# One order of tensor work in an attention, a third early slot in the expert layer behind it, and an earlier last turn in its small slots

## The chip, the cores and the metric

The kernel runs on one core of one Trainium2 chip. The metric is the device time of one execution in microseconds (us), taken as the median of several runs. The profile shows one more execution of the same program.

## The reference

An attention over buckets, and behind it a layer of eight experts of which each token uses one. For the attention there are 4 batches of 8 heads, 768 positions and 64 dimensions; each query and key gets a 6-bit bucket from the signs of a projection, and scores count only between equal buckets.

```
q_bits = einsum("bhsd,dk->bhsk", q, proj) > 0          # k_bits likewise; 6 bits make a bucket
scores = where(q_bucket == k_bucket, 0.125 * q @ k.T, -1e9)
scores = scores - max(scores)
attn   = exp(scores) / (sum(exp(scores)) + 1e-9)
x      = (attn @ v) as [3072 tokens, 512]
logits = x @ w_gate + modality_bias[modality_id]       # 8 experts
e      = argmax(logits);  gate_w = softmax(logits)[e]
out[t] = gate_w[t] * (relu(x[t] @ w1[e]) @ w2[e])      # w1: 512 x 1024, w2: 1024 x 512 per expert
```

All inputs are random and float32; the results are float32 too.

## The kernel before

**Attention.** The 32 heads are worked as 16 pairs, four pairs to a batch. For one pair, TensorE turns the loaded q and k (tiles n) to the layout that it multiplies, makes the hash bits, and adds to the turned q and k rows of patterns, so that a score of unequal buckets comes out far below the others. The work of the pair i is spread over six steps kt (blocks of 128 keys), and work for other pairs is woven in. In which order PE gets the pieces is written by hand: `PLAN` has a string for each kt, and a letter is one piece of work. The letters that matter here:

- S: one step of the scores of pair i (L306 and L307 into the PSUM tile pss, exponentials on ACT in L319 and L324 into pb). A: weighing of the values (L342 into psu).
- M: one step of the row maxima of pair i+1 (L240 into psm; DVE reduces it to mx in L242). B: its way back (L269, a turn into psx, and DVE's L271 and L272, which write m_1g and lone from it).
- T: one step of the chain for pair i+2: turns of n (L181, four 128 x 128 transposes into psx), signs (L208), patterns (L223). P: the same chain of the pair before.
- f, g, e, h, k: steps of `finish` of the last batch (normalisation, logits, routing). x, y: steps of `finish_x` (turn of the batch's result in L423, DVE's L425 into xs, a store of xs to the DRAM tile x_d in L427).

The pools of psx, psm and pss have two buffers each. A string's order is PE's order; the other engines are ordered by a scheduler.

**Routing.** When a batch's attention is done, `finish` computes logits and gates, and counts tokens by expert (L608 on PE, DVE's L590 to L627); POOL scatters (L630) token numbers and gates into the DRAM table tab, sorted by expert. Tokens are worked in slots: a big slot is 256 tokens of one expert, a small one 128. Slots that need only the first three batches are called early; their experts and offsets are in the table eslot, made by `early_slots()`. When all four batches are routed, `late_slots()` (L641 to L712) makes the tables bslot and sslot for the rest. `EARLY` is the number of early slots, `SURE_BIG` = 12 - EARLY the number of late big slots that run without a guard, and two small slots run without one. Further slots, if the tokens need them, run behind branches in `conditional`.

**A slot.** `Runner.slot` has eight steps j. At each, `ahead()` issues weight loads (SP, L747 for w1 and L749 for w2, 512 KB each into four raw buffers; up to seven steps ahead) and splits what has come in into a high and a low part (ACT casts in L755, DVE or POOL subtracts in L757, w with seven buffers). Each product is done as three matmuls of the parts. Steps 0 to 3 are the first product (L792 to L794 into hps, ACT's L798, DVE's L799), steps 4 to 7 the second (L834 to L836 into yps); at the end y is scaled (ACT, L841) and scattered to the output (POOL, L842).

A slot's tokens are fetched by `gather`: SP reads the slot's offset (L762) and issues a read of its part of tab into tb (L765); POOL, when tb is there, issues one gather for each 128 tokens (L769) from x_d into xg. `prepare` turns xg (L780, eight transposes for a big slot) and splits it into xh and xl (L781, L782). `prepare` of the next slot stands at j = 4; `fetch` of the next two slots (fd = 2) at j = 0 of every slot but the first.

In a small slot, the first product comes out with tokens in the partitions (L808 to L810), ACT makes hn (L812), and `turn_small` turns it (L818, two transposes), with a copy on ACT (L821, hh) and a subtraction on DVE (L822, hl). There are four turns, one step behind the products; the last is at j = 4.

`drive` weaves generators: the slot's eight steps, and beside them a given number of steps of another generator, spread over a given part. The small slots are at places 10 and 13 of the 14, counted from 0.

Of the kernel before, what the change touches and what calls it, by code (L numbers as in the profile page):

```python
# [9 lines left out]
F32 = mybir.dt.float32  # L10
# [4 lines left out]
ALU = mybir.AluOpType  # L15
# [3 lines left out]
B, H, S, D = 4, 8, 768, 64  # L19
# [3 lines left out]
REST = S - MAIN  # L23
NP = B * H // 2
BIG = 2.0 ** 100
CFG = dict(spd=(15,), fxs=3, wy=(0.3, 0.71), hpf=0, he=0, hn=0, hm=0, avp=(1, 2, 3, 4, 5, 6), avs=(2,), early=2, w3=(0, 0.9), x3=(0, 1), nmd=1, man=(), man0=2, hpo=0, hpe=0, p0=(0, 1), p1=(0, 0.25), p2=(0, 0.4), p3=(0.4, 0.9), s0=4, rc='DDDD', rq=(1, 2), tq=(3, 3, 1, 1, 0, 0), wh=(0.5, 0.78), ws=(0.78, 1.05), n2=2, psx=2, psm=2, pss=2, npb=4, ut=8, qk=3, v=2, wm=(0, 0.9), wf=(0.04, 1.02), wx=(0.3, 0.71), sub="DPPD", fx='D', fx3='R', raw=4, wp=7, LS=4, LL=7, pn=8, rv=(0,), rs='DDPP', r1=(0, 0.5), r2=(0, 1), avg=1, fub=2, fd=2, pm=(), fj=0, fxe=1.0)
P = 128

LAG = 2
PLAN = (  # L30
    "LvSPMTMSASfMTMfexyhk",
    "SMTVMSASfMTMeyghk",
    "SMTMSAQFGlSMTMEfxyk",
    "SMSATWSBMEekk",
# [23 lines left out]
def drive(gens):  # L58

    at = [0] * len(gens)  # L60
    alive = [True] * len(gens)
    while any(alive):
        j = min((x for x in range(len(gens)) if alive[x]), key=lambda x: gens[x][2] + (gens[x][3] - gens[x][2]) * (at[x] + 1) / gens[x][1])
        try:
            next(gens[j][0])
            at[j] += 1
        except StopIteration:
            alive[j] = False
# [7 lines left out]
def attention(ctx, actx, tc, a, x_d, l_d, route=None, setup=None):  # L76
# [4 lines left out]
    spool = ctx.enter_context(tc.tile_pool(name="spool", bufs=2))  # L81
    upool = ctx.enter_context(tc.tile_pool(name="upool", bufs=CFG["ut"]))
    bp = ctx.enter_context(tc.tile_pool(name="bp", bufs=1))
    ps_x = ctx.enter_context(tc.tile_pool(name="ps_x", bufs=CFG["psx"], space=PSUM))
    nat = actx.enter_context(tc.tile_pool(name="nat", bufs=CFG["n2"]))
    ld = actx.enter_context(tc.tile_pool(name="ld", bufs=CFG["qk"]))
    gens = []
    for g in range(3):
        opp = actx.enter_context(tc.tile_pool(name=f"opp{g}", bufs=1))
        gens.append({n: [opp.tile([P, S], F32R, name=f"{n}_{h}g{g}") for h in range(2)] for n in ("m1", "s1", "m2", "s2")})  # L90
    ldv = actx.enter_context(tc.tile_pool(name="ldv", bufs=CFG["v"]))
    sm = actx.enter_context(tc.tile_pool(name="sm", bufs=4))
    const = actx.enter_context(tc.tile_pool(name="const", bufs=1))
    ps_m = actx.enter_context(tc.tile_pool(name="ps_m", bufs=CFG["psm"], space=PSUM))
    ps_s = actx.enter_context(tc.tile_pool(name="ps_s", bufs=CFG["pss"], space=PSUM))
# [427 lines left out]
EARLY = CFG["early"]  # L523
# [194 lines left out]
def experts(ctx, tc, a, x_d, tab, out, ps_x, ident):  # L718
    nc = tc.nc
    w1, w2 = a["moe_w1"], a["moe_w2"]  # L720
    xp = ctx.enter_context(tc.tile_pool(name="xp", bufs=2))
    raw = ctx.enter_context(tc.tile_pool(name="raw", bufs=CFG["raw"]))
# [11 lines left out]
    def nt(s):  # L734
        return 1 if s[0] == "s" else 2
# [49 lines left out]
    def gemm1(hi, lo, xh, xl, hh, hl):  # L785
        hi = hi.rearrange("p (c f) -> p c f", c=4)
        lo = lo.rearrange("p (c f) -> p c f", c=4)
        for fb in range(2):
            fs = slice(fb * P, (fb + 1) * P)
            hps = ps_h.tile([P, TS], F32, name="hps")  # L790
            for c in range(4):
                nc.tensor.matmul(hps, lo[:, c, fs], xh[:, c], start=(c == 0), stop=False)  # L792
                nc.tensor.matmul(hps, hi[:, c, fs], xl[:, c], start=False, stop=False)  # L793
                nc.tensor.matmul(hps, hi[:, c, fs], xh[:, c], start=False, stop=(c == 3))  # L794
            th = hp.tile([P, TS], F32R, name="hh")
            tl = hp.tile([P, TS], F32R, name="hl")
            with tc.high_priority(offset=CFG["hpo"]):
                nc.scalar.activation(th, hps, AF.Relu)  # L798
                nc.vector.scalar_tensor_tensor(out=tl, in0=hps, scalar=0.0, in1=th.bitcast(F32), op0=ALU.max, op1=ALU.subtract)  # L799
            hh.append(th)  # L800
            hl.append(tl)
# [13 lines left out]
    def turn_small(h, hh, hl):  # L815
        tp = ps_h.tile([P, TS], F32, name="hps")
        for fb in range(2):
            nc.tensor.transpose(tp[:, fb * P:(fb + 1) * P], h[:, fb * P:(fb + 1) * P], ident)  # L818
        th = hp.tile([P, TS], F32R, name="hh")
        tl = hp.tile([P, TS], F32R, name="hl")  # L820
        nc.scalar.copy(out=th, in_=tp)  # L821
        nc.vector.tensor_tensor(out=tl, in0=tp, in1=th.bitcast(F32), op=ALU.subtract)  # L822
        for fb in range(2):
            hh.append(th[:, fb * P:(fb + 1) * P])
            hl.append(tl[:, fb * P:(fb + 1) * P])

    def gemm2(j, hi, lo, hh, hl, yps):
        hi = hi.rearrange("p (c f) -> p c f", c=2)
        lo = lo.rearrange("p (c f) -> p c f", c=2)
        for fb in range(2):  # L830
            fc = (j - 4) * 2 + fb
            for g in range(len(yps)):
                gs = slice(g * P, (g + 1) * P)
                nc.tensor.matmul(yps[g], hl[fc][:, gs], hi[:, fb], start=(fc == 0), stop=False)  # L834
                nc.tensor.matmul(yps[g], hh[fc][:, gs], lo[:, fb], start=False, stop=False)  # L835
                nc.tensor.matmul(yps[g], hh[fc][:, gs], hi[:, fb], start=False, stop=(fc == 7))  # L836
# [8 lines left out]
    class Runner:  # L845
# [35 lines left out]
        def slot(self, k):  # L881
            s = self.order[k]
            nxt = self.order[k + 1] if k + 1 < len(self.order) else None
            self.prepare(s)
            hh, hl, h = [], [], None
            for j in range(8):
                self.ahead()
                if j == CFG["fj"] and k > 0:
                    for s2 in self.order[k + 1:k + 1 + CFG["fd"]]:
                        self.fetch(s2)  # L890
                if j == 4:
                    yps = [ps_y.tile([P, DM], F32, name="yps") for _ in range(nt(s))]
                    if nxt:
                        self.prepare(nxt)
                hi, lo = self.ws.pop(self.n)
                if j >= 4:
                    gemm2(j, hi, lo, hh, hl, yps)
                elif nt(s) == 2:
                    gemm1(hi, lo, *self.xs[s], hh, hl)
                else:  # L900
                    last, h = h, gemm1_small(hi, lo, *self.xs[s])
                    if last is not None:
                        turn_small(last, hh, hl)
                if j == 4 and h is not None:
                    turn_small(h, hh, hl)
                self.n += 1
                yield
            store(self.got[s][0], yps)
# [22 lines left out]
def body(tc, a, out):  # L931
    nc = tc.nc
    x_d = tc.dram_tile([N + 1, DM], F32, name="x_d")
    tab = tc.dram_tile([DUMMY + TS, 2], I32, name="tab")
    with ExitStack() as ctx, ExitStack() as actx:
        route, early_slots, late_slots, setup = router(ctx, tc, a, x_d, tab)
        finish, finish_x, ps_x, ident = attention(ctx, actx, tc, a, x_d, None, route, setup)
        actx.close()
        runner, tabs, conditional = experts(ctx, tc, a, x_d, tab, out, ps_x, ident)
        r = runner()  # L940
        with tc.high_priority(offset=CFG["hpf"]):
            tabs["e"] = early_slots()
        r.extend([("e", i) for i in range(EARLY)])
        with tc.high_priority(offset=CFG["hpf"]):
            r.fetch(("e", 0))
        with tc.high_priority(offset=CFG["hpe"]):
            r.prepare(("e", 0))
        r.ahead()
        r.fetch(("e", 1))
        k = 0  # L950
        if EARLY > 2:
            drive([(r.slot(0), 8, 0, 1), (finish(B - 1), 14, *CFG["w3"])])
            drive([(r.slot(1), 8, 0, 1), (finish_x(B - 1, 0, NT), 12, *CFG["x3"])])
            k = 2
        else:
            for _ in finish(B - 1):
                pass
        tabs["b"], tabs["s"], tot = late_slots()
        late = [("b", i) for i in range(SURE_BIG)]
        for i in range(SURE_SML):  # L960
            late.insert(len(late) - 3 * i, ("s", i))
        r.extend(late)
        if EARLY == 2:
            drive([(r.slot(0), 8, 0, 1), (finish_x(B - 1, 0, NT), 12, 0, CFG["fxe"])])
            k = 1
        for k in range(k, len(r.order)):
            drive([(r.slot(k), 8, 0, 1)])
        conditional(tot)
# [13 lines left out]
```

## Time and profile before

| what | value |
|---|---|
| time, three runs | 877.72, 882.26, 884.44 us (median 882.26) |
| profiled execution | 876.72 us, span 874.9 us, mean granted TensorE clock 0.985 |
| PE busy | 817.9 us (93%) |
| DVE, ACT, POOL busy | 585.8, 506.0, 458.6 us |
| DMA | 110.87 MB, mean 127 GB/s |

The span is what the profiler saw between the first and the last instruction; the execution's time has 1.8 us around it. The attention lasts to about 535 us, and the 14 slots follow. In rows of the timeline the columns are start, duration, engine, line and operation, the result and its sources, shapes, the count, and in brackets the idle time before and what ended it. In rows of waits they are the waiting engine, tile and line, what it waited for, and total us, number, longest. SPq and POOLq are the queues in which SP and POOL issue their transfers.

### The profile page before, as it was taken

How to read it: one execution, taken by the hardware profiler on the slowest of the kernel's cores; microseconds unless marked ns; L12 is line 12 of the kernel's file. 1: busy time of each engine (PE TensorE's matmuls, PEld its weight loads, DVE VectorE, ACT ScalarE, POOL GpSimd, SP SyncE). 2: the span in 40 equal slices, each digit the busy share in tenths (PEclk: the TensorE clock that was granted, in tenths of full speed). 3: DMA queues.
4: the chain of work that ended last, by engine and by line, in shares of the span. 5: the costliest groups of instructions: out<-in, count | busy, mean ns of one | idle time of the engine just before them, and what ended most of it. 6: DMA issues, size and time to landing. Idle time of an engine off the chain costs nothing.

```text
span 874.9 us, 14548 instructions
## 1 busy us (share of the span) xinstructions
PE 817.9 (93%) x5154; PEld 579.5 (66%) x5154; DVE 585.8 (67%) x1029; ACT 506.0 (58%) x953; POOL 458.6 (52%) x347
## 2 busy tenths in 40 slices
PE   6799999999999999999999898879999999999993
PEld 3556555555555654555554555779999999998993
DVE  6776676676967676977677876954656565657550
ACT  4566666665666665666665464444555555557551
POOL 5387678657669857669757687322222221123010
PEclk9899999999999999999999999999999999999997
DMA  6423213212325221324210164796777777778750
GB/s 170 116 67 84 70 34 85 74 47 62 98 61 97 74 64 45 99 66 72 55 46 10 31 229 121 166 253 199 235 223 215 232 220 215 221 230 276 228 158 22
DMA packets 76753, 110.87 MB, mean 127 GB/s; under 512 B 10495, under 2 KB 52095, under 8 KB 76672
## 3 DMA queue, kind: packets, MB, share of 16 engines
q1 hardware_dynamic: 70880, 95.14, 39.2%
q0 software_dynamic: 4928, 13.14, 4.1%
q10 hardware_dynamic: 864, 1.57, 0.9%
q8 instruction: 43, 0.70, 0.4%
q14 instruction: 38, 0.31, 0.1%
HBM read 84.83 MB, written 13.33 MB: 112 GB/s over the span
## 4 chain that ended last, share of the span: by engine, by line
PE 74%; DVE 11%; DMA 4%; ACT 4%; issue 3%; POOL 2%; SPq 0%; POOLq 0%; DVEq 0%; ACTq 0%
PE psu L342 13%; PE pss L306 8%; PE pss L307 6%; PE yps L834 5%; PE yps L836 5%; PE yps L835 5%; PE psm L240 5%; PE hps L794 4%; PE hps L793 4%; PE hps L792 4%; PE psx L181 3%; PE psx L208 3%; PE psm L246 3%; POOL sp L327 2%; DVE mx L242 1%
## 5 line engine op out<-in xcount | busy, mean ns | idle before, releaser
L327 POOL TENSOR_TENSOR sp<-sp,pb 128x768 f32<-128x768 f32 x124 | 225.5, 1844 | 43.6 <-ACT pb L324 42.1
L757 DVE TENSOR_TENSOR w<-raw,w 128x1024 fp32r<-128x1024 f32 x108 | 134.9, 1251 | 94.4 <-ACT w L755 93.7
L755 ACT CAST w<-raw 128x1024 fp32r<-128x1024 f32 x112 | 117.1, 1048 | 61.9 <-PE yps L836 55.3
L242 DVE TENSOR_REDUCE mx<-psm 128x1 f32<-128x512 f32 x192 | 127.9, 686 | 32.0 <-PE psm L240 28.1
L342 PE MATMUL psu<-pb,vt 128*64 128x512 f32 (+1 forms) x768 | 145.6, 500 | 0.0
L319 ACT ACTIVATE pb<-pss 128x512 f32<-128x512 f32 x192 | 114.9, 599 | 40.6 <-PE pss L307 30.1
L324 ACT ACTIVATE pb<-pss 128x512 f32<-128x512 f32 x96 | 57.5, 599 | 127.1 <-PE pss L307 121.6
L792 PE MATMUL hps<-xh,w 128*128 128x256 f32 x384 | 108.9, 284 | 2.6 <-issue 1.6
L793 PE MATMUL hps<-xl,w 128*128 128x256 f32 x384 | 108.9, 284 | 0.0
L794 PE MATMUL hps<-xh,w 128*128 128x256 f32 x384 | 108.5, 283 | 0.0
L342 PEld LDWEIGHTS psu<-pb,vt 128*64 128x64 f32 x768 | 46.8, 136 | 86.4 <-issue 86.1
L769 POOL DMA_INDIRECT xg<-x_d,tb x26 | 31.6, 1214 | 124.6 <-DMA tb<-tab 99.5
L842 POOL DMA_INDIRECT out<-y,tb x26 | 34.5, 1328 | 117.7 <-ACT y L841 61.0
L834 PE MATMUL yps<-w,hl 128*128 128x512 f32 x208 | 83.4, 401 | 1.3 <-DVE hl L822 1.3
L836 PE MATMUL yps<-w,hh 128*128 128x512 f32 x208 | 81.8, 393 | 0.0
L835 PE MATMUL yps<-w,hh 128*128 128x512 f32 x208 | 81.6, 393 | 0.0
L248 DVE TENSOR_REDUCE mx<-psm 128x2 f32<-128x512 f32 x96 | 66.1, 689 | 22.9 <-PE psm L246 21.5
L306 PE MATMUL pss<-m_0g,s_0g 128*128 128x512 f32 x192 | 78.0, 406 | 0.0
L792 PEld LDWEIGHTS hps<-xh,w 128*128 128x128 f32 x384 | 73.4, 192 | 3.9 <-issue 1.8
L793 PEld LDWEIGHTS hps<-xl,w 128*128 128x128 f32 x384 | 73.6, 192 | 1.7 <-issue 1.2
L794 PEld LDWEIGHTS hps<-xh,w 128*128 128x128 f32 x384 | 73.5, 192 | 0.0
L167 POOL TENSOR_TENSOR n<-qk,n 128x384 fp32r<-128x384 f32 x36 | 40.2, 1122 | 56.9 <-ACT n L163 48.0
(214 smaller groups left out, 1767.3 us busy)
## 6 DMA issues: line engine op xcount, KB each, us to landing
raw<-moe_w SPq DMA_DIRECT2D x112, 512.0 KB
qk<-q SPq DMA_DIRECT2D x32, 192.0 KB
qk<-k SPq DMA_DIRECT2D x32, 192.0 KB
vt<-v SPq DMA_DIRECT2D x16, 384.0 KB
x_d<-xs SPq DMA_DIRECT2D x18, 256.0 KB
m_1g<-m_1g SPq DMA_DIRECT2D x16, 192.0 KB
s_1g<-s_1g SPq DMA_DIRECT2D x16, 192.0 KB
m_0g<-m_0g SPq DMA_DIRECT2D x15, 192.0 KB
```

The source lines that it names most:

```text
L242: nc.vector.tensor_reduce(out=mx[:, qt + j, hi, 0:1], in_=mp, axis=AX.X, op=ALU.max)
L306: nc.tensor.matmul(out, t["s1"][h][:, ks], t["m1"][h][:, cs], start=True, stop=False)
L327: (nc.vector if h and i in CFG["spd"] else nc.gpsimd).tensor_tensor(out=t["sp"][:, h], in0=(t["pb"][0] if kt == 1 else t["sp"])[:, h], in1 ...
L342: nc.tensor.matmul(t["u"][part][64 * h:64 * h + 64, 0:w], t["v"][:, h, kt], t["pb"][kt][:, h, COLS[part]], start=False, stop=(kt == NT - 1 ...
L755: nc.scalar.copy(out=hi, in_=r)
L757: (nc.gpsimd if pool else nc.vector).tensor_tensor(out=lo, in0=r, in1=hi.bitcast(F32), op=ALU.subtract)
L792: nc.tensor.matmul(hps, lo[:, c, fs], xh[:, c], start=(c == 0), stop=False)
L793: nc.tensor.matmul(hps, hi[:, c, fs], xl[:, c], start=False, stop=False)
L794: nc.tensor.matmul(hps, hi[:, c, fs], xh[:, c], start=False, stop=(c == 3))
L834: nc.tensor.matmul(yps[g], hl[fc][:, gs], hi[:, fb], start=(fc == 0), stop=False)
L835: nc.tensor.matmul(yps[g], hh[fc][:, gs], lo[:, fb], start=False, stop=False)
L836: nc.tensor.matmul(yps[g], hh[fc][:, gs], hi[:, fb], start=False, stop=(fc == 7))
```

## The change

Four edits. The first string of `PLAN` has T behind the second M and the second S instead of in front of them. `early` goes from 2 to 3: one more slot is taken from the first three batches and one fewer from the rest (`SURE_BIG` 10 to 9). With more than two early slots, a branch of `body` that was there already runs: `finish` of the last batch is woven into slot 0 and `finish_x` into slot 1, and `late_slots` comes after slot 1. All early slots but the first are fetched ahead of slot 0, and the later fetches begin in the last early slot, in the middle of it (j = 4), and from then on at j = 0. In small slots, the last turn stands in front of the next slot's `prepare`, and the copy and subtraction of every turn get a higher priority with the scheduler.

```diff
-CFG = dict(... hpf=0, he=0, ... early=2, w3=(0, 0.9), x3=(0, 1), ...)
+CFG = dict(... hpf=0, hs=60, he=0, ... early=3, w3=(0, 0.9), x3=(0, 1), ...)
 PLAN = (
-    "LvSPMTMSASfMTMfexyhk",
+    "LvSPMMSTASfMTMfexyhk",
...
     def turn_small(h, hh, hl):
...
-        nc.scalar.copy(out=th, in_=tp)
-        nc.vector.tensor_tensor(out=tl, in0=tp, in1=th.bitcast(F32), op=ALU.subtract)
+        with tc.high_priority(offset=CFG["hs"]):
+            nc.scalar.copy(out=th, in_=tp)
+            nc.vector.tensor_tensor(out=tl, in0=tp, in1=th.bitcast(F32), op=ALU.subtract)
...
             for j in range(8):
                 self.ahead()
-                if j == CFG["fj"] and k > 0:
+                if j == (4 if k < EARLY else 0) and k >= EARLY - 1:
                     for s2 in self.order[k + 1:k + 1 + CFG["fd"]]:
                         self.fetch(s2)
                 if j == 4:
+                    if h is not None:
+                        turn_small(h, hh, hl)
+                        h = None
                     yps = [ps_y.tile([P, DM], F32, name="yps") for _ in range(nt(s))]
                     if nxt:
                         self.prepare(nxt)
...
-                if j == 4 and h is not None:
-                    turn_small(h, hh, hl)
...
-        r.fetch(("e", 1))
+        for i in range(1, EARLY):
+            r.fetch(("e", i))
         k = 0
         if EARLY > 2:
             drive([(r.slot(0), 8, 0, 1), (finish(B - 1), 14, *CFG["w3"])])
             drive([(r.slot(1), 8, 0, 1), (finish_x(B - 1, 0, NT), 12, *CFG["x3"])])
```

PE's order in one pair of the attention, the piece of the difference (psm, pss, psu and psx are the PSUM tiles of above; - is before, + the change):

```order
-L240 MATMUL psm<-s_0g_102,m_0g_100 128x512
-L181 MATMUL psx<-identr,n_1340 128x128 x4
-L240 MATMUL psm<-s_0g_102,m_0g_100 128x512
+L240 MATMUL psm<-s_0g_102,m_0g_100 128x512 x2
 L306 MATMUL pss<-m_1g_123,s_1g_125 128x512
 L307 MATMUL pss<-m_1g_127,s_1g_129 128x512
+L181 MATMUL psx<-identr,n_1340 128x128 x4
 L342 MATMUL psu_1277<-pb_178,vt 64x512 x2
```

The four turns went behind one maxima step and one score step.

SP's order where the first late slot b0 is fetched. Before, the reads of the tables of b0 and b1 (L765) are behind the last w2 load of the slot in front, and ahead of the first w1 load (L747) of b0:

```order
L749 DMA raw<-moe_w 128x2x512
L762 TENSOR_LOAD bslot
L765 ISA
L765 DMA tb<-tab 128x4
L762 TENSOR_LOAD bslot
L765 ISA
L765 DMA tb<-tab 128x4
L739 TENSOR_LOAD bslot
L747 ISA
L747 DMA raw<-moe_w 128x4x256
```

In the changed kernel:

```order
L739 TENSOR_LOAD bslot
L747 ISA
L747 DMA raw<-moe_w 128x4x256
L747 ISA
L747 DMA raw<-moe_w 128x4x256
L747 ISA
L747 DMA raw<-moe_w 128x4x256
L747 ISA
L747 DMA raw<-moe_w 128x4x256
L762 TENSOR_LOAD bslot
L765 ISA
L765 DMA tb<-tab 128x4
```

The table's read moved behind the four w1 loads of b0.

PE's order in the first small slot, at the end of its first product, before:

```order
L810 MATMUL hps<-w,xh 128x256
L818 MATMUL hps<-ident,hn 128x128 x2
L780 MATMUL psx<-ident,xg 128x128 x8
L834 MATMUL yps<-w,hl 128x512
L835 MATMUL yps<-w,hh 128x512
L836 MATMUL yps<-w,hh 128x512
L834 MATMUL yps<-w,hl 128x512
L835 MATMUL yps<-w,hh 128x512
L836 MATMUL yps<-w,hh 128x512
L818 MATMUL hps<-ident,hn 128x128 x2
```

and in the changed kernel, whose lines from 821 on are numbered one higher or more:

```order
L810 MATMUL hps<-w,xh 128x256
L818 MATMUL hps<-ident,hn 128x128 x2
L780 MATMUL psx<-ident,xg 128x128 x2
L818 MATMUL hps<-ident,hn 128x128 x2
L780 MATMUL psx<-ident,xg 128x128 x6
L835 MATMUL yps<-w,hl 128x512
```

The last turn (the second L818) moved from behind six matmuls of the second product into the midst of the next slot's transposes.

More of the change, by code (lines that the diff above doesn't have):

```diff
@@ L25 @@
 BIG = 2.0 ** 100
-CFG = dict(spd=(15,), fxs=3, wy=(0.3, 0.71), hpf=0, he=0, hn=0, hm=0, avp=(1, 2, 3, 4, 5, 6), avs=(2,), early=2, w3=(0, 0.9), x3=(0, 1), nmd=1, man=(), man0=2, hpo=0, hpe=0, p0=(0, 1), p1=(0, 0.25), p2=(0, 0.4), p3=(0.4, 0.9), s0=4, rc='DDDD', rq=(1, 2), tq=(3, 3, 1, 1, 0, 0), wh=(0.5, 0.78), ws=(0.78, 1.05), n2=2, psx=2, psm=2, pss=2, npb=4, ut=8, qk=3, v=2, wm=(0, 0.9), wf=(0.04, 1.02), wx=(0.3, 0.71), sub="DPPD", fx='D', fx3='R', raw=4, wp=7, LS=4, LL=7, pn=8, rv=(0,), rs='DDPP', r1=(0, 0.5), r2=(0, 1), avg=1, fub=2, fd=2, pm=(), fj=0, fxe=1.0)
+CFG = dict(spd=(15,), fxs=3, wy=(0.3, 0.71), hpf=0, hs=60, he=0, hn=0, hm=0, avp=(1, 2, 3, 4, 5, 6), avs=(2,), early=3, w3=(0, 0.9), x3=(0, 1), nmd=1, man=(), man0=2, hpo=0, hpe=0, p0=(0, 1), p1=(0, 0.25), p2=(0, 0.4), p3=(0.4, 0.9), s0=4, rc='DDDD', rq=(1, 2), tq=(3, 3, 1, 1, 0, 0), wh=(0.5, 0.78), ws=(0.78, 1.05), n2=2, psx=2, psm=2, pss=2, npb=4, ut=8, qk=3, v=2, wm=(0, 0.9), wf=(0.04, 1.02), wx=(0.3, 0.71), sub="DPPD", fx='D', fx3='R', raw=4, wp=7, LS=4, LL=7, pn=8, rv=(0,), rs='DDPP', r1=(0, 0.5), r2=(0, 1), avg=1, fub=2, fd=2, pm=(), fj=0, fxe=1.0)
 P = 128
```

## The prediction

> **What bounds the kernel now.** I read the page's first part: which engine is busy.
>
> ```profile
> PE 817.9 (93%) x5154; PEld 579.5 (66%) x5154; DVE 585.8 (67%) x1029; ACT 506.0 (58%) x953; POOL 458.6 (52%) x347
> ```
>
> TensorE works 93% of the span, so a change that takes no matmul away can only win back PE's idle time and its half-clock time. Where that lies, the windows by stage show (columns: window, length, then busy time and instructions of PE, PEld, DVE, ACT, POOL, the granted clock, DMA share, GB/s).
>
> ```profile
> 534.94:602.13 67.19, 58.40 (x382) 49.30 (x382) 47.73 (x117) 28.90 (x45) 21.75 (x18) 0.97 0.74 196
> 589.87:602.13 12.26, 12.26 (x51) 10.04 (x49) 5.06 (x5) 4.36 (x6) 0.71 (x1) 0.89 0.51 182
> 648.75:672.05 23.30, 23.30 (x154) 21.40 (x152) 14.04 (x18) 13.17 (x21) 5.33 (x5) 1.00 0.75 225
> 661.06:672.05 10.99, 10.99 (x52) 9.10 (x50) 6.35 (x7) 5.35 (x7) 0.96 (x1) 1.00 0.70 202
> 497.04:500.45 3.41, 3.41 (x17) 2.05 (x14) 0.36 (x2) 1.16 (x3) 3.24 (x5) 0.50 0.01 0
> 589.20:592.60 3.40, 3.40 (x13) 2.82 (x12) 1.38 (x2) 1.17 (x2) 0.00 (x0) 0.50 1.00 391
> ```
>
> A steady big slot (648.75 to 672.05) has PE busy all its 23.30 us: nothing to win. The passage from the attention to the steady slots (534.94 to 602.13) idles 67.19 - 58.40 = 8.8 us. Twice the clock was 0.50 for 3.4 us. The waits of PE name the idle time: first its largest group in the attention, then everything from 536 us on (total us, times, longest).
>
> ```profile
> PE psx L181 <- DVE lone L272: 6.4, 12, 0.5
> ...
> PE psx L780 <- DMA xg<-x_d,tb: 3.4, 2, 2.0
> PE hps L792 <- issue: 1.6, 1, 1.6
> PE psx L780 <- DVE xs L425: 1.3, 1, 1.3
> PE yps L834 <- DVE hl L822: 1.3, 1, 1.3
> PE hps L792 <- DVE hl L799: 1.0, 2, 0.6
> PE psx L384 <- DVE gsb L376: 0.7, 1, 0.7
> PE psx L608 <- DVE oh L603: 0.6, 1, 0.6
> ```
>
> The L822 row lies in the first small slot, all the others from 536 us on in the passage. The change's three parts touch three places: the T groups (L181), the passage, and the small slot.
>
> **Part 1, the T groups behind an M and an S.** One of the twelve places, PE and then DVE:
>
> ```profile
> 250.92 0.53 PE L240 MATMUL psm<-s_0g,m_0g 128*128 128x512 f32 x1
> 251.99 0.50 PE L181 MATMUL psx<-identr,n 128*128 128x128 f32 x4 [0.53 <-DVE lone L272]
> 252.33 0.46 PE L240 MATMUL psm<-s_0g,m_0g 128*128 128x512 f32 x1
> 252.63 0.39 PE L306 MATMUL pss<-m_1g,s_1g 128*128 128x512 f32 x1
> 252.86 0.40 PE L307 MATMUL pss<-m_1g,s_1g 128*128 128x512 f32 x1
> 253.18 0.65 PE L342 MATMUL psu<-pb,vt 128*64 128x512 f32 x2
> ```
>
> ```profile
> 251.42 0.42 DVE L272 TENSOR_SCALAR lone<-psx 128x256 fp32r<-128x256 f32 x1
> 251.87 0.55 DVE L224 CAST m_1g<-psx 64x384 fp32r<-64x384 f32 x1
> 252.46 0.69 DVE L242 TENSOR_REDUCE mx<-psm 128x1 f32<-128x512 f32 x1
> ```
>
> The ends of matmuls are modelled, so I count from start to start. An L240 gives way to the next matmul after 0.30 us (252.33 to 252.63); the first one here, begun at 250.92, would have done so at 251.22, but the transposes began at 251.99, when L272 (251.42 + 0.42 = 251.84) had let their psx buffer go. So 0.77 us is lost, not the 0.53 printed. The M and S now put in front are 252.33 to 253.18, 0.85 us of work. Started at 251.22, they end at 252.07, which is 0.08 later than 251.99: the wait is just covered. Can they start early? M's psm buffer can: DVE's L242 had not begun on the first psm at 252.33, when the second was already being filled, so that one was free before. S's pss buffer is taken back by L324, whose cost I leave to a rival. DVE's work neither grows nor shrinks. With so thin a cover I take 0.75 of the 0.77, 12 x 0.75 = **9.0 us**; bounds 6.4 (the printed idle time alone) and 9.2.
>
> **Part 2, three early slots.** Gone from the path is the first passage: before, the last batch's finish ran alone on PE (the waits on L376 and, with slot 0, on L425's stores). Now it lies beside slot 0 and the copy of its result beside slot 1, with matmuls to fill in. No matmul is added or dropped: 14 slots run before, and by the reference's routing of its own inputs 14 run after. (Three batches give experts 1 and 3 1124 and 1099 tokens, 4 + 4 full blocks of 256, enough for three early slots; the totals of 1477, 1469, 98 and 28 need 12 big and 2 small slots.) The two fetches that are issued ahead instead of one cost SP and POOL their issue (rows of L765 and L769 below: 0.35 us and 1.3 us each), beside the finish, with POOL's next weight not used until a slot later; their cover is the whole of slot 0, and I count nothing.
>
> Of the 5.2 us of waits in the passage that are not gathers, I let three stay, since their producers are all still there, beside slots: oh 0.6, hl 1.0, xs 1.3, together 2.9. The other two go (0.7 + 1.6 = 2.3). Bounds: all 5.2 stay, or all go.
>
> Then the gather of b0. Before, it is fetched for slot 1, and PE waited 3.4 us for it (in two pieces, the longest 2.0); right behind it comes the half-clock window of 589.20. What that costs stands in the windows above: the second half of that slot, from its first L834, took 12.26 us, that of a steady slot 10.99, so 1.27 us. In the changed kernel b0 is fetched in the middle of slot 2, and on SP its table stands behind the four L747 loads of its weights. A steady slot has those loads at the same place on SP:
>
> ```profile
> 645.85 8.95 SPq L747 DMA_DIRECT2D raw<-moe_w  x4
> 657.31 9.49 SPq L749 DMA_DIRECT2D raw<-moe_w  x4
> 667.38 0.35 SPq L765 DMA_DIRECT2D tb<-tab  x1
> ```
>
> Then POOL in the same slot, the time from issue to landing of all 26 gathers (view of line L769), and PE where it needs the rows:
>
> ```profile
> 671.09 1.60 POOL L769 DMA_INDIRECT xg<-x_d,tb  x1 [11.80 <-DMA tb<-tab]
> 673.00 0.97 POOL L769 DMA_INDIRECT xg<-x_d,tb  x1 [0.30 <-issue]
> ```
>
> ```profile
> DMA to landing us min/median/max: 3.7/3.9/4.0
> ```
>
> ```profile
> 660.27 1.03 PE L780 MATMUL psx<-ident,xg 128*128 128x128 f32 x8
> ```
>
> With S the start of the slot (648.75 here): the fourth L747 is issued by 654.80, S + 6.05. A table read follows a load by 667.38 - 666.80 = 0.58, so S + 6.63; POOL's first gather starts 3.71 behind it, the second 1.91 later, and lands 3.9 after that: S + 16.15. PE is at the transposes of the next slot at S + 11.52 (660.27) and, with one group of gemm2 in front (some 0.7 us), needs the rows at S + 12.2 to 12.3. So a **new wait of about 3.8 us** stands where 3.4 stood. Bounds: nothing (if SP reaches the table before its weight loads have filled their buffers) and 5.7 (one more POOL issue of 1.91 in front); I take 3.8, as it is made of rows of the very queues.
>
> Whether the half-clock window follows decides 1.27 us more. The trace has one such window behind 3.4 us of waiting and one (497.04, row above) behind a wait that the row of its first matmul gives as 1.73 us:
>
> ```profile
> 495.57 0.50 PE L240 MATMUL psm<-s_0g,m_0g 128*128 128x512 f32 x1 [1.73 <-DVE mx L242]
> ```
>
> A wait of 3.8 us is longer than both, so I charge the window again. The Trainium skill, "TensorE: Matmul & The Clock Gate", Part 1, has the rate halved after at least one whole idle window of about 3.4 us. By that rule neither the 1.73 us wait nor the 3.4 us in two pieces should have triggered anything; the trace shows half rate behind both, so the measurement decides. By the page a new wait in two pieces would cost no clock, and the sum below would be 13.3 in place of 12.0, inside the forecast's own range.
>
> Net for part 2: 2.3 + (3.4 - 3.8) + (1.27 - 1.27) = **1.9 us**. Bounds: -2.3 (the five others stay and the new wait is 5.7) and 5.2 + 3.4 + 1.27 = 9.9.
>
> **Part 3, the small slot.** ACT in the small slot's second half, before:
>
> ```profile
> 794.62 0.39 ACT L812 ACTIVATE hn<-hps 128x256 f32<-128x256 f32 x1
> ...
> 797.37 1.05 ACT L755 CAST w<-raw 128x1024 fp32r<-128x1024 f32 x1 [2.10 <-DMA raw<-moe_w]
> ...
> 800.23 0.39 ACT L821 CAST hh<-hps 128x256 fp32r<-128x256 f32 x1
> ```
>
> PE at the third turn's transposes:
>
> ```profile
> 794.36 0.38 PE L818 MATMUL hps<-ident,hn 128*128 128x128 f32 x2
> ```
>
> The fourth L821 stands behind a weight cast that waited 2.10 us for its load, and PE waits 1.3 us for what follows it (the L822 row). Now it is issued in front of these. The 1.3 goes. In its place the fourth turn's transposes wait for L812, which ends at 794.62 + 0.39 = 795.01, and PE, with only two L780 transposes between, comes to them sooner. The third turn's transposes began at 794.36 and these and two more take some 0.2 each, as 2 of the 8 of the L780 row take 0.26: PE is there at about 794.8, so about 0.25 is lost. Net **1.1 us** (bounds 0.5, if the copies hold up the next slot's L781, and 1.3). The other small slot is the last of all and has no next slot to prepare: nothing.
>
> **Sum.** 9.0 + 1.9 + 1.1 = 12.0 us against this execution's 876.72 (span 874.9): 864.7. The execution shown is the fastest of four (877.72, 882.26, 884.44 are the others; mean 880.3), so I take 12.0 from the mean: **868.3 us**. From the median it would be 870.3. A measurement of this kernel can tell about 1% (8.8 us) from no change.
>
> **Rivals.**
>
> *The passage gives nothing, or costs.* xs has two buffers, so each of the copies three to six waits for the store two before it. DVE serves in order: behind a waiting L425 stand the weights' L757 and the L799 of slot 1, for which PE waits; on ACT, whose queue issues the stores, its L798. From the chain:
>
> ```profile
> 564.99 8.14 DMA x_d<-xs
> ```
>
> Six groups in a slot of 23.30 us are 3.9 us apart, or 3.3 where the spread leaves a step at the ends empty, and two of them 6.5 to 7.8. If each store takes 8.14, each of four copies may cost up to 1.6 us, 6.4 instead of the 1.3 that I left: 5.1 lost, gain 6.9. With the other two waits still there (2.3) it is 4.6. That is 873 to 876. For it: the 1.6 and 1.3 us waits before are of this kind. Against it: this is the longest piece of the chain there and need not be the rule, and the three hps buffers let PE run on for a while. Chance 0.20.
>
> *The wait before T only moves.* If S's pss isn't free when PE comes 0.77 us sooner, or if T still finds psx taken because L271, L272 slip as well, part 1 gives nothing and 3.0 stay: 877. For it: only 0.08 us of slack. Against it: DVE begins L271 and L272 with nothing of the moved groups in front. Chance 0.10.
>
> *The gather comes in time.* If SP reaches b0's table early, the 3.8 and the window's 1.27 go: gain 17, **863**. For it: the loads at that place could be issued before their buffers fill. Against: in steady slots they aren't. Chance 0.10.
>
> *Slower.* The number of unguarded big late slots falls from 10 to 9. If the third early slot finds no full block, or more than nine late ones are needed, a guarded slot runs behind a branch: a slot of 23.30 us, not overlapped with the loads of its weights, 8 x 512 KB = 4.19 MB, which at the steady 225 GB/s take 18.6 us. That is +42 before the gain of 12, **about 910**. It decides from 3 full blocks by the third batch; by the reference's routing there are 8. Chance 0.05, and in it whatever else costs a per cent.
>
> **How the numbers follow.** The forecast itself has 0.55; its own range, 864 to 873, lies nearly all on the faster side (873.4 is 1% below the median), so 0.50 faster and 0.05 same. Of the passage's 0.20, 0.02 are faster and 0.18 same; the moved wait's 0.10 are same; the early gather's 0.10 faster. Faster 0.62, same 0.33, slower 0.05. Range: all bounds on their good side give 9.2 + 9.9 + 1.3 = 20.4, 860 from the mean, less the scatter of the runs (2.6 below their mean, rounded): 858. All on the other side give 6.4 - 2.3 + 0.5 = 4.6, so 876; the moved wait (877) and the same scatter take the far end to 880.
>
> **What would show it.** In the attention's waits the L181 row on lone falls from 6.4 to under 1; if my first part fails, there is a like sum on L240 or L306. In slot 2 two waits of L780 on xg sum to about 3.8, with a window at clock 0.5 behind them; tb's issue stands behind four L747. In slots 0 and 1, waits of 2.9 on oh, hl, xs; 6 or more on L799 or L425 means the first rival. In the first small slot no wait on L822, and about 0.25 on L812. What would make it all wrong is a second-order effect in the attention's DVE order that I can't see from PE's rows, over twelve pairs.

## The result and the profile after

The changed kernel took 874.19 us (median of 14 runs, 871.09 to 877.61), the kernel before beside it 878.83 us (14 runs, 872.33 to 884.44). The ratio is 0.9942, 95% interval 0.9916 to 0.9967: 0.6% faster, about 5 us, where 12 us were forecast. The profiled execution took 875.23 us, with a span of 873.4 us and a mean granted clock of 0.976 (before 0.985).

The two profiled executions differ by only 1.5 us, so I read from them where time came from and where it went, and leave the size of the whole to the ratio. PE at the end of the attention, in the changed kernel, and in the second row in the kernel before:

```profile
528.20 1.51 PE L360 MATMUL psx<-sp,ones 128*32 128x384 f32 x8 [2.66 <-POOL sp L327]
534.94 0.85 PE L360 MATMUL psx<-sp,ones 128*32 128x384 f32 x8 [1.17 <-POOL sp L327]
```

By this L360 the attention is 6.74 us shorter. In the kernel before, the passage from there to the start of the fourth slot took 90.50 us (columns as in the prediction's windows):

```profile
534.94:625.44 90.50, 81.71 (x533) 70.70 (x534) 61.77 (x135) 42.06 (x65) 27.21 (x22) 0.98 0.74 204
```

The same passage after, with PE's same 533 matmuls, and the first small slot and the slot behind it:

```profile
528.20:624.35 96.15, 86.74 (x533) 74.18 (x534) 61.88 (x135) 42.15 (x64) 30.28 (x22) 0.90 0.67 192
787.03:800.35 13.32, 13.22 (x89) 12.01 (x88) 9.27 (x12) 10.72 (x19) 4.37 (x4) 1.00 0.85 285
800.35:824.61 24.26, 23.55 (x153) 21.45 (x152) 16.88 (x21) 14.45 (x22) 2.24 (x2) 1.00 0.79 247
```

The passage is 5.65 us longer, not 1.9 shorter. Its idle time is 9.41 us (before 8.79), but PE's busy time for the same matmuls grew by 5.03 us: the mean clock there is 0.90 instead of 0.98. The small slot is 1.30 shorter (14.62 before) and the slot behind it 0.97 longer (23.29 before). 6.74 - 5.65 + 0.33 = 1.4 is all that the two profiles differ by.

The waits of PE from 526 us on, after:

```profile
PE psx L780 <- DVE xs L425: 5.9, 1, 5.9
PE psx L780 <- DMA xg<-x_d,tb: 3.3, 1, 3.3
PE psx L360 <- POOL sp L327: 2.7, 1, 2.7
PE hps L792 <- DVE hl L799: 0.7, 1, 0.7
PE psx L608 <- DVE oh L603: 0.2, 1, 0.2
```

Of the six rows of waits that the passage had before (8.6 us in all, the longest single wait 2.0), two large ones and 0.2 us for oh are left. The row of L360 lies just in front of the passage, that of L799 in the slot behind the small slot. And each of the three large rows has low clock behind it (windows of the changed kernel at those places):

```profile
527.59:534.42 6.83, 6.22 (x28) 2.85 (x29) 3.13 (x5) 3.63 (x5) 3.46 (x3) 0.50 0.33 79
578.79:585.62 6.83, 4.79 (x14) 3.92 (x15) 3.12 (x4) 1.01 (x2) 1.00 (x1) 0.50 0.86 302
609.51:616.34 6.83, 5.92 (x18) 4.96 (x19) 1.33 (x2) 1.23 (x3) 1.32 (x2) 0.50 0.61 211
```

20.5 us at half rate stand against 3.4 in the same stretch before. The first of the three stretches is behind the wait for sp at the end of the attention, not behind a wait of the early slots. 6.22 us of it lie in the passage, with PE busy throughout; at half rate that costs half, so an estimated 3.1 of the 5.65 us. The wait for L425, DVE in slot 1:

```profile
572.86 0.69 DVE L425 TENSOR_TENSOR xs<-psx,rin 128x512 f32<-128x512 f32 x1 [1.98 <-DMA x_d<-xs]
573.47 1.22 DVE L757 TENSOR_TENSOR w<-raw,w 128x1024 fp32r<-128x1024 f32 x1
574.60 0.75 DVE L799 SCALAR_TENSOR_TENSOR hl<-hps,hh 128x256 fp32r<-128x256 f32 x2
580.09 0.69 DVE L425 TENSOR_TENSOR xs<-psx,rin 128x512 f32<-128x512 f32 x1 [4.74 <-DMA x_d<-xs]
```

The third and the fourth L425 wait for the store two before; the fourth holds the psx buffer that the second half of e2's transposes needs. The stores that these two waited for were issued at 562.82 and 569.12, about 10 and 11 us earlier. The wait for the gather, SP and POOL at b0's fetch in slot 2, which began at 594.78:

```profile
590.96 9.87 SPq L747 DMA_DIRECT2D raw<-moe_w  x4
601.37 0.35 SPq L765 DMA_DIRECT2D tb<-tab  x1
```

```profile
606.28 0.98 POOL L769 DMA_INDIRECT xg<-x_d,tb  x1 [5.00 <-DMA tb<-tab]
```

As forecast, the table is read behind four L747, here at S + 6.6 (S is the start of the slot); POOL starts at S + 11.5, where S + 10.3 was forecast.

In the attention, the twelve waits of L181 for lone are gone. In their place the waits of the stretch 46 to 534 us have these two rows, which before had 0.2 in one and none in the other:

```profile
PE psm L246 <- DVE mx L242: 1.4, 3, 0.6
...
PE psm L240 <- DVE mx L248: 0.7, 2, 0.4
```

### The profile page after: what moved, and what is told of

Same layout as the page of the kernel before. It is cut to its first block, busy times and chain, and to the rows that moved or that the text cites. A ratio compares the mean times of both kernels' runs of the same rounds, so it can differ in the third digit from the quotient of the medians.

```text
span 873.4 us, 14545 instructions
## 1 busy us (share of the span) xinstructions
PE 818.9 (94%) x5154; PEld 583.5 (67%) x5154; DVE 587.9 (67%) x1029; ACT 506.0 (58%) x953; POOL 461.1 (53%) x347
## 4 chain that ended last, share of the span: by engine, by line
PE 74%; DVE 10%; DMA 5%; ACT 4%; issue 3%; POOL 3%; SPq 0%; POOLq 0%; DVEq 0%; ACTq 0%
PE psu L342 13%; PE pss L306 8%; PE pss L307 6%; PE yps L835 5%; PE yps L837 5%; PE psm L240 5%; PE yps L836 5%; PE hps L792 4%; PE hps L793 4%; PE hps L794 4%; PE psx L208 3%; PE psx L181 3%; PE psm L246 3%; DMA x_d<-xs 2%; DVE w L757 2%
## 5 line engine op out<-in xcount | busy, mean ns | idle before, releaser
L757 DVE TENSOR_TENSOR w<-raw,w 128x1024 fp32r<-128x1024 f32 x108 | 136.9, 1268 | 92.6 <-ACT w L755 92.3
L242 DVE TENSOR_REDUCE mx<-psm 128x1 f32<-128x512 f32 x192 | 127.9, 686 | 32.0 <-PE psm L240 30.2
L837 PE MATMUL yps<-w,hh 128*128 128x512 f32 x208 | 82.8, 398 | 0.0
L836 PE MATMUL yps<-w,hh 128*128 128x512 f32 x208 | 82.4, 396 | 0.0
L248 DVE TENSOR_REDUCE mx<-psm 128x2 f32<-128x512 f32 x96 | 66.1, 689 | 15.3 <-PE psm L246 13.8
L798 ACT ACTIVATE hh<-hps 128x256 fp32r<-128x256 f32 x96 | 36.6, 383 | 58.6 <-PE hps L794 45.3
```

Of the source, the lines that this page charges most:

```text
L242: nc.vector.tensor_reduce(out=mx[:, qt + j, hi, 0:1], in_=mp, axis=AX.X, op=ALU.max)
L757: (nc.gpsimd if pool else nc.vector).tensor_tensor(out=lo, in0=r, in1=hi.bitcast(F32), op=ALU.subtract)
```

## The experiments

My theory after the result was this: the T groups brought nearly what was forecast; the third early slot gave it back, through the two waits and, more than by their length, through the clock behind them. The rivals: the attention brought less and the early slots cost nothing; the wait for the stores is really one for busy DMA engines; the gather must wait for the stores anyway; the clock is only a side effect.

**The string of PLAN alone** (the kernel before, first string as in the change).

> The kernel before with the new first string of PLAN alone. Theory (the attention part is worth nearly what was forecast, and the passage gives it back): the last pair but one ends some 8.2 us earlier as in the changed kernel (its L360 at about 510.5 instead of 518.7), 6 to 8 us faster than before, ratio 0.991 to 0.993. Rival (the moved T groups only push the wait to L246, L306 and the sums of the last pair): no more than 4 us, ratio 0.995 or above.

Measured: 870.57 us (6 runs), ratio 0.9909 (0.9881 to 0.9937). From the first pair's L360 to that of the pair numbered 12, the profile has 374.39 us, the kernel before 381.01, the changed kernel 374.33. By the medians this edit alone gives more than the whole change, though the intervals overlap. The size that the theory gave holds (8.0 us by the ratio). The time that I had named for it in the trace doesn't: the last L360 but one came at 513.45, not at 510.5. The step in front of it takes 29.8 us here and 28.6 to 29.9 in nine other profiles, but 27.8 in that of the kernel before and 27.0 in that of the changed one, so these two are the odd draws.

**Three early slots alone** (the change without the string and without the small slot's part).

> The changed kernel with the old string of PLAN and the old place and priority of the small slot's last turn: three early slots and the fetches ahead alone. Theory: the passage is some 4 to 6 us longer than before (a wait of 5 to 6 us for L425, one of 3 us for the gather of b0, each with low clock behind it), ratio 1.004 to 1.007. Rival (three early slots cost nothing, and the attention part brought less than it shows): ratio 0.998 to 1.001.

Measured: 883.12 us (12 runs), ratio 1.0053 (1.0025 to 1.0081): slower. Its waits from 500 us on:

```profile
PE psx L780 <- DVE xs L425: 6.4, 2, 5.0
PE psx L780 <- DMA xg<-x_d,tb: 3.3, 1, 3.3
```

The two waits are the early slots' own, with or without the rest of the change. Here, where the wait for sp was 0.7 us and no low clock followed it, the passage takes 93.45 us, 2.95 more than before:

```profile
536.57:630.02 93.45, 83.34 (x533) 72.40 (x534) 61.64 (x135) 42.94 (x65) 29.55 (x22) 0.93 0.68 197
```

**Six xs buffers** in the changed kernel, taken from the expert layer's memory:

```diff
-            xs = bp.tile([P, 512], F32, name="xs", bufs=2)
+            xs = a["xsp"].tile([P, 512], F32, name="xs6") if b == B - 1 else bp.tile([P, 512], F32, name="xs", bufs=2)
...
-    yp = ctx.enter_context(tc.tile_pool(name="yp", bufs=4))
+    yp = ctx.enter_context(tc.tile_pool(name="yp", bufs=4)); a["xsp"] = ctx.enter_context(tc.tile_pool(name="xsp", bufs=6))
```

> The changed kernel with six buffers instead of two for the last batch's xs, so that no L425 waits for a store two before it. Theory (the stores hold DVE, and DVE holds PE): the 5.9 us wait of L780 for L425 goes, with 1 to 2 us of low clock: 6 to 8 us faster than the changed kernel, about 867. Rival (the DMA engines are behind with the weights there, and PE would wait for raw instead): 2 us or less, about 872.

Measured: 868.68 us (6 runs), ratio to before 0.9896 (0.9867 to 0.9924): some 4 us faster than the changed kernel, less than expected. The wait for L425 is gone, and slot 1 takes 27.7 us instead of 34.5. But PE now comes to b0's rows sooner and waits longer there, and slot 2 takes 31.5 us instead of 29.6:

```profile
PE psx L780 <- DMA xg<-x_d,tb: 5.1, 2, 4.0
```

The rival is out here: no wait for weights took the place. That the stores themselves are slow is true all the same (median us from issue to landing in the last column; the first row are the earlier batches' stores, the second those beside the weight loads; they differ in the queue too, so it isn't shown that the loads alone slow them):

```profile
x_d<-xs SPq DMA_DIRECT2D x18, 256.0 KB, 2.2
x_d<-xs ACTq DMA_DIRECT2D x6, 256.0 KB, 8.0
```

**b0 fetched at the start of slot 2** in the changed kernel, ahead of its weight loads:

```diff
-                if j == (4 if k < EARLY else 0) and k >= EARLY - 1:
+                if j == 0 and k >= EARLY - 1:
```

> The changed kernel with b0 and b1 fetched at the start of the last early slot (j = 0), ahead of the weight loads of b0 on SP, instead of in the middle. Theory (the table's place on SP makes the wait): the 3.3 us wait of L780 for the gather goes, with 1 to 2 us of low clock: 4 to 5 us faster than the changed kernel, about 869.5. Rival (the gather must wait for the last stores of x_d, which land about then anyway): 0 to 2 us.

Measured: 871.67 us (6 runs), ratio 0.9918 (0.9886 to 0.995), 2 us faster than the changed kernel, with intervals that overlap: that is the rival's size. But in the profile, slot 2 takes 23.30 us instead of 29.57, with no wait for the gather, as the theory has it; what hid it is slot 1, which took 36.8 us in that execution, with more waiting for the stores:

```profile
PE psx L780 <- DVE xs L425: 7.6, 2, 3.8
```

The rival's mechanism cost PE nothing: the last store was issued at 595.10 and landed 3.3 us later, POOL's first gather for b0 began at 599.65, and that is still only 2.7 us into the slot.

**Both together.**

> The changed kernel with both: six xs buffers and b0 fetched at the start of the last early slot. Theory (the two waits are separate): 5 to 6 us faster than with the six buffers alone (868.7), about 863, no wait over 1 us between the attention and the late slots. Rival (with the first wait gone, PE comes to b0's transposes 7 us sooner, before the last stores and the gather can be done): about 867, a wait of 2 us or more for xg stays.

Measured: 862.45 us (6 runs), ratio 0.9824 (0.9799 to 0.985). Here is the passage and its waits:

```profile
527.60:608.57 80.97, 78.91 (x533) 69.17 (x534) 61.13 (x135) 42.63 (x65) 29.63 (x22) 1.00 0.77 228
```

```profile
PE pss L306 <- ACT pb L324: 1.9, 3, 1.4
PE psx L423 <- DVE xl L782: 1.7, 1, 1.7
```

The passage takes 80.97 us, 15.2 less than in the changed kernel, and the clock is full; of the 15.2, an estimated 3.1 are the low clock behind the wait for sp, which is 0.7 us here. The time is the theory's; one wait of 1.7 us stayed in the passage, where it had none above 1. This is the best version of all, 1.8% faster than before and, by the ratios, some 10 us faster than the change as made. That is more than the 4 and 2 us of the single steps, but each of these sizes has an interval of some 3 us to either side.

**Two early slots, with the string and the small slot's part.**

> The kernel before with the new string of PLAN and the earlier last turn in small slots, with two early slots as before. Theory (the third early slot is what costs): 869 to 871, as with the string alone or 1.3 us faster, some 4 us faster than the whole change. Rival (early slots and string work on each other): 874 as with the whole change.

Measured: 871.7 us (6 runs), ratio 0.992 (0.9898 to 0.9941), the same as the string alone within the intervals. So the third early slot as made costs about 2 us here, with intervals that overlap; with the old string it cost 0.5%, clear of the noise.

**The same with six xs buffers.**

> The same, with six xs buffers. It shows what the third early slot is worth with the stores' wait gone in both. Theory: the waits of before for L425 and its kin (1.3 + 1.6) go, 866 to 868; the third early slot is then worth 3 to 5 us with its fetch moved, and nothing or less without. Rival (the third early slot is worth nothing even then): 863 to 864, as the version with three early slots and both mended.

Measured: 872.06 us (6 runs), ratio 0.9925 (0.9905 to 0.9946). The buffers bring nothing here; I had expected 866 to 868 us. PE waits for other things in place of the stores:

```profile
PE hps L792 <- DVE hl L799: 5.4, 3, 3.5
PE psx L780 <- DMA xg<-x_d,tb: 2.5, 1, 2.5
```

Without the buffers the row of L799 has 5.5 us, as much. But what stands behind its longest wait is another thing. Without them DVE waits for a store (first row); with them ACT waits for a weight load, and DVE's L757 and L799 follow (second row, of the run with the buffers):

```profile
568.88 1.29 DVE L425 TENSOR_TENSOR xs<-psx,rin 128x512 f32<-128x512 f32 x2 [6.12 <-DMA x_d<-xs]
570.92 1.04 ACT L755 CAST w<-raw 128x1024 fp32r<-128x1024 f32 x1 [4.34 <-DMA raw<-moe_w]
```

With two early slots it is thus as the rival of the first run with six buffers has it: a wait for weights takes the place.

So with its two waits mended the third early slot is worth 0.9925 to 0.9824, about 9 us, more than I had expected; without, it costs.

**The small slot's part alone**, one run.

> The kernel before with the earlier last turn in small slots alone; one look for its waits. Theory: the wait of L834 for L822 (1.3 us in the profile before, 1.9 with the string alone) is gone, a wait of L818 for L812 of 0.1 to 0.3 us is there, the small slot takes 13.3 us instead of 14.6; a wait of about 0.7 us of L792 for L799 in the slot behind appears or not whatever the small slot does. Rival: that 0.7 us comes from the earlier turn.

Measured: 884.4 us in one run, too few to tell. The small slot takes 13.47 us. The slot behind took 25.20 us, with this wait in it:

```profile
814.92 0.39 PE L792 MATMUL hps<-xh,w 128*128 128x256 f32 x1 [1.66 <-DVE hl L799]
```

The wait goes with the earlier turn, as the rival has it: of the eight profiles with the new turn, seven have it, with 0.5 to 1.7 us (the eighth has 0.9 us for L812 in the small slot), and of the four with the old turn none. The string alone, which has the old turn, has 24.30 us there without any such wait, because a half-rate window (793.96 to 797.37) reaches into the slot; the three others have 23.29. Over both slots together, the four profiles with the old turn have 37.91, 38.29, 38.60 and 40.05 us, the eight with the new one 37.40 to 38.67, median 37.9. By the medians it brings some 0.6 us, less than the profiles scatter; half or more of what the turn wins comes back as the wait for L799 in the next slot. Why that product is late, I have not tested.

**Matmuls to fill the waits** (the changed kernel; the added results are overwritten).

```diff
+                    for _ in range({1: 24, 2: 12}.get(k, 0)):
+                        nc.tensor.matmul(yps[0], hh[0][:, 0:P], self.ws[self.n][0][:, 0:DM], start=True, stop=True)
                     if nxt:
                         self.prepare(nxt)
```

> The changed kernel with idle matmuls added (their result is overwritten): 24 of 128x512 in the middle of slot 1 and 12 in the middle of slot 2, ahead of the next slot's transposes, 5.4 and 2.7 us at full clock, less than the two waits of 5.9 and 3.3 us. Theory (most of what the passage lost is not the waits but the half clock that follows them): the low-clock windows of slots 1 and 2 disappear or halve, the matmuls behind the waits run at full speed, and with 36 matmuls more the kernel is 4 to 5 us faster than the changed one, about 869.5. Rival (the waits alone are the loss and the clock is a side effect): no gain, 874 to 875, or 8 us slower if the waits don't absorb the added work.

Measured: 876.34 us (12 runs), ratio 0.9964 (0.9936 to 0.9991): no gain, no clear loss. The passage and its two low windows:

```profile
528.18:625.43 97.25, 90.81 (x569) 78.54 (x570) 62.55 (x135) 42.97 (x65) 29.49 (x22) 0.96 0.67 190
581.73:585.14 3.41, 3.41 (x11) 2.83 (x10) 2.10 (x3) 1.17 (x2) 0.00 (x0) 0.50 0.87 285
612.45:615.86 3.41, 3.41 (x12) 2.85 (x11) 1.39 (x2) 1.17 (x2) 0.00 (x0) 0.50 0.62 243
```

The two low stretches behind the waits halved, as the theory had it, but the time didn't fall. The sum: 36 matmuls at 0.227 us are 8.2 us more; PE's busy time rose by only 4.1 (90.81 - 86.74), so the better clock gave back 4.1; the idle time fell from 9.41 to 6.44, by 3.0. 8.2 - 4.1 - 3.0 = 1.1, which is 97.25 - 96.15. My expectation failed in taking the waits' ends as fixed: the transposes behind the first came at 22.2 us into slot 1 instead of 20.6. Most of the 4.1 isn't these two windows: the wait for sp at the end of the attention was 0.7 us in this execution, with no low clock behind, and that is an estimated 3.1. So this run doesn't show that the clock, more than the waits, is what the third early slot lost; how the loss divides between them rests on the estimates of the next section.

**T behind the second M alone**, one run.

> The kernel before with T behind the second M alone, still in front of the second S; one look at the attention. Theory (the work put in front covers the wait, start for start): an M is 0.30 us, so the twelve waits for lone fall from 0.53 to about 0.24 us as printed (6.4 to about 2.9), and the attention is some 3.6 us shorter than before, about half of what the full move gave. Rival (it is the freed buffers or the changed order on DVE that brought it): waits gone as with the full move, or not shorter at all.

Measured: 878.09 us in one run. The waits in the attention:

```profile
PE psm L240 <- DVE mx L242: 3.7, 2, 2.0
PE psx L181 <- DVE lone L272: 3.6, 12, 0.3
```

The printed wait falls from 0.53 to 0.30 a place. From the first pair's L360 to that of pair 12 it took 379.35 us, 1.7 less than before, where the full move gave 6.7. The ordinary pairs gain 0.2 to 0.27 us instead of 0.73 to 0.81. So the work put in front does cover the wait, and less work covers less of it; but the 3.6 us that I expected became 1.7, since an M's worth here is 0.23, not 0.30, and the two pairs that gained nothing with the full move lose 0.22 and 0.25.

## Why the prediction was wrong

**Part 1 was right in its mechanism, a little high in size.** The L181 row is gone. By the L360 of each pair, ten of the twelve places gave 0.73 to 0.81 us (forecast 0.75); the two pairs numbered 5 and 9 gave nothing (33.86 and 33.83 us after, 33.72 and 33.71 before). There PE now waits for a psm buffer that DVE still reduces (the two psm rows above; at one place L240 0.35 us for L248 and L246 0.55 us for L242). The wait only moved there, which is the second rival's outcome by another buffer: the prediction took psm as free from one place of the twelve. Together 7.4 instead of 9.0 us.

**Part 2 is the step that failed, in two terms.** First, "I let three stay ... together 2.9": oh and hl came to 0.2 (forecast 1.6), but xs to 5.9 (forecast 1.3). That is the first rival's mechanism: two buffers, slow stores, DVE in order. It was given 0.20 and a time of 873 to 876, and 874.2 came out. That the time fits is partly luck, since the rival had four waits of up to 1.6 us and no loss by the clock, and took part 1 at 9.0. I had the row of 8.14 us and put it down as a longest piece that need not be the rule; the two stores that DVE waited for took some 10 and 11 us, and the stores' median beside the weight loads is 6.2 to 11.1 us in the four profiles that list it. Second, "(1.27 - 1.27)": the low clock was taken as an equal term on both sides. PE's busy time for the passage's 533 matmuls is 78.9 us at full clock (both waits mended), 81.7 before, 86.7 after. Most of the differences is clock. Of the 5.0 us between before and after, an estimated 3.1 lie behind the wait for sp and are no part of the early slots. The two stretches behind the early slots' waits have 4.79 and 5.92 us of busy time at half rate, an estimated 5.4 lost, against 1.7 of the one window of before: 3.7 lost where I counted none. With the 3.1 that makes 6.8, more than the 5.0 seen, so these estimates are good to some 2 us: PE's modelled ends at the waits count as busy time too, about 1 us of them before.

The gather's wait came out near, 3.3 for 3.8, with its place on SP, but in part by luck: POOL began 1.2 us later than forecast, and PE's wait ended at 610.42, 4.1 us after the first gather began, so with the rows of the first, where the sum had those of the second. In all, the passage lost 5.65 us where +1.9 was forecast; without the 3.1 behind the wait for sp it is 2.5, close to the 2.95 of three early slots alone.

The Trainium skill, "TensorE: Matmul & The Clock Gate", Part 1, says that the window is free-running. With that the traces agree: the three low stretches above begin 15 and 9 windows of 3.41 us apart. That the rate is halved only after a whole idle window they do not bear out (last section); by that rule the sum would have been 13.3, farther off.

**Part 3** was right on its wait (L822's row is gone; L818 waited 0.10 us for L812 where I had 0.25) and wrong in what comes next: the slot behind took the gain back, 0.33 left of 1.30 in this profile, some 0.6 over all, which is less than the scatter.

**The others.** The guarded slot didn't run (14 slots in the trace). The wait at the last pair I didn't see: its L360 waited 2.66 us for sp instead of 1.17. In the ten other profiles, five of them with three early slots, that row is 0.7; so I take it for scatter of the execution, not for the change. By terms: 7.4 for 9.0, -2.5 for 1.9 (without the stretch behind sp), 0.3 to 0.6 for 1.1. That is about 5, as the 14 runs of each have it; the two profiles differ by only 1.4, for the 3.1 of that stretch and 0.7 at the last pairs come off.

## What to carry to other kernels

Before a copy is moved beside another slot, look at how long its stores take there and how many buffers they hold: over two buffers a wait of 1.3 us became one of 5.9 when the stores took 10 and 11 us. Price a wait of PE of about 2 us or more with the half-rate stretch that may follow. Count the waits of a chain together: with the first mended alone the second grew (slot 2 took 31.5 us instead of 29.6), and with both mended the kernel gained some 10 us. With two early slots, more buffers only let a wait for weights take the stores' place. A table read that a gather needs belongs ahead of the bulk loads on its queue: slot 2 took 23.30 us so instead of 29.57.

## What the runs showed of the hardware

PE's clock followed a fixed grid of 3.41 us windows. I laid it over the PE rows of the eleven profiles that have low clock between 46 and 845 us; idle time is counted with PE's modelled ends. All 19 full-rate windows with 1.9 us or more idle were followed by half rate; of the seven with 1.72 to 1.84 us, four were; none with less. The twelfth profile, with both waits mended, has no low clock there and no window with more than 1.65 us idle. So about half a window of idle time was enough, and a wait that straddles two windows can cost nothing: a wait of 1.96 us for mx, 4.8 us behind the L360 of pair 12, lay 0.76 and 1.20 us in two windows before and changed nothing, and fell into one window in four other profiles and halved the next. The rate came back only behind a low window with at most 0.5 us idle: six low windows with 0.6 to 1.1 us idle were followed by another.

The scatter of the times goes with the clock, though which of the two brings the other isn't shown. Of the changed kernel's 14 runs, the four fastest (871.09 to 871.62 us) have a mean clock of 0.981 to 0.984, the three slowest (877.14 to 877.61) 0.974 to 0.978.
